# Tap sums on TensorE, filter copies shared with VectorE, sine tables between rows and Wo copies behind the x stores: a long convolution beside a recurrent attention

## The chip, the cores and the metric

The kernel runs on one core of a Trainium2 chip. The metric is device time in microseconds (us), the median of several executions; a profile of one execution gives its time by engine. Engines are TensorE (PE, with its weight loads as PEld), VectorE (DVE), ScalarE (ACT), GpSimd (POOL) and SyncE (SP). DMAs are issued from the queues of SP, ACT and POOL.

## The reference, cut to what matters

Two independent results lie side by side in the output: `A` in columns 0 to 1023, `B` in columns 1024 to 2047. Everything is bf16, with one batch and 2048 positions.

```python
# A: q, k, v [2048, 1024], shift_k [1024, 4], ssm_k [1024, 2048], ssm_D [1024]
k_pad   = pad(k, 3 zero rows in front)
k_shift = sum over t of k_pad[t:t+2048, :] * shift_k[:, 3-t]      # four taps of k
kv      = k_shift * v
y       = causal convolution over positions of kv with ssm_k (by FFT of length 4096)
A       = q * (y + kv * ssm_D)

# B: x [2048, 1024], mem0 [8, 1024], Wq, Wk, Wv [1024, 32 heads, 128], Wo [32, 128, 1024]
for s in range(64):                      # segments of 32 positions
    h = concat(mem, x[s])                # 8 + 32 rows
    q, k, v = h@Wq, h@Wk, h@Wv
    o = (masked softmax(q k^T / sqrt(128)) v) @ Wo
    mem, B[s] = o[:8], o[8:]             # the memory rows go on to the next segment
```

## The kernel before, in words

The program has two parts. `a_kernel` computes `A` in three stages and, while it does so, calls back into `b_kernel`, which prepares data for the 64 segments; then `b_kernel` runs the segments one after the other (from about 430 us to the end), streaming weights from a DRAM copy `WS`.

**Stage 1** (inside `with ExitStack() as c1`) runs 16 rows `t`. A row takes the 128 positions t, t+16, ... of all 1024 channels. In each row:

- eight TensorE transposes (L236) bring one slice of the filter `ssm_k` into PSUM (`k_tp`), and ScalarE copies it to SBUF as `kt` (L238). For row 0 VectorE adds `ssm_D` into it (L240);
- `stage1(kt, t, SK1)` multiplies it by two DFT matrices `F1h` (L220, four matmuls into two PSUM tiles `s_ps`, a pool of two), ScalarE copies each of the two results to SBUF (`s_sb`, L222, a pool of three), and SP stores them to DRAM (L223);
- `k` and `v` for two rows at a time are loaded in even rows (L244 on SP, L247 on POOL);
- VectorE forms the four taps of `k`: one product (L253), then three products (L256) each added to the sum `uacc` (L257), and multiplies the sum by `v` (L259) to `u`;
- `stage1(u, t, SU1)` does with `u` what was done with `kt`.

Before the rows come small tables, and among them four big sine tables that only stage 2 reads: `Mre` and `Mim` (L200 to L206), `Nre` and `Nim` (L207 to L213). VectorE forms the integer phases in a scratch tile `ints`, ScalarE applies Sin (in `act_sin`, L109), and POOL zeroes one stripe of each of `Mre` and `Mim` (L206).

`stage1_done` (L482) follows the rows: it transposes part of `x` into `XBT` (`make_xbt`; X loads held behind the stores of rows 3 to 6, its PSUM tiles from the pool `b_ps0`, tag `ps0`, two buffers) and runs `dense(0, 0)`, 16 times eight matmuls (L594) into `kb_ps`, which are also `ps0` tiles.

**Stage 2** has 17 sets of two units each; a unit gathers spectra of `u` and of the filter, multiplies them (DVE L327 to L330 and L334, POOL L333) and transforms back. **Stage 3** has 16 steps and writes `A`. After each of these 34 + 16 pieces `a_kernel` calls `fill()` (L629), which does one piece of `b_kernel`'s preparation: a store of finished projections, an x block (`x_block`, L565, with its store to `REC` on POOL at L575), one projection's matmuls, and, from piece `WO_COPY` = 27 on, one copy of a chunk of `Wo` to `WS`, from DRAM to DRAM, issued on POOL (L637). There are six such copies.

Outside the segments the order of the instructions on each engine is not that of the source: the framework sorts them by priority (order in the source) and readiness under its own model, hands out tile buffers as it goes, and fixes one order for each engine. `tc.issue_after(ins)` pins the instructions issued inside it behind `ins` in the order of the queue they share. The copies at L637 have nothing that they wait for, so they may be placed ahead of the piece that they were written in.

Of the kernel before, what the change touches and what calls it, by code (L numbers as in the profile page):

```python
# [9 lines left out]
BF = mybir.dt.bfloat16  # L10
F32 = mybir.dt.float32
I32 = mybir.dt.int32
ACT = mybir.ActivationFunctionType
ALU = mybir.AluOpType
# [16 lines left out]
PITCH = 2048  # L31


def a_kernel(ctx: ExitStack, tc, q, k, v, shift_k, ssm_k, ssm_D, outa, slot16, stage1_done, fill):
    nc = tc.nc
    S, D = 2048, 1024
    NP = 34
# [8 lines left out]
    ident = const.tile([128, 128], BF, name="a_ident")  # L46
    F1h = [const.tile([128, 128], BF, name=f"F1h{h}") for h in range(2)]
    G2h = [const.tile([128, 128], BF, name=f"G2h{h}") for h in range(2)]
    Mre = const.tile([128, NP, 64], BF, name="Mre")
    Mim = const.tile([128, NP, 64], BF, name="Mim")  # L50
    Nre = const.tile([128, NS, 128], BF, name="Nre")
    Nim = const.tile([128, NS, 128], BF, name="Nim")
# [4 lines left out]
    with ExitStack() as c1:  # L57
# [3 lines left out]
        wk = c1.enter_context(tc.tile_pool(name="a1_wk", bufs=3, side="right"))  # L61
# [46 lines left out]
        def act_sin(out_ap, a_int_ap, nbits, p0=0):  # L108
            nc.scalar.activation(out_ap, a_int_ap, ACT.Sin, bias=pi_col[p0:p0 + out_ap.shape[0], 0:1],  # L109
                                 scale=-2.0 * PI / (1 << nbits))  # L110
# [56 lines left out]
        SH = cw.tile([128, 4, 1024], BF, name="SH")  # L167
        for hf in range(4):
            pt = ps_big.tile([128, 1024], F32, tag="big", name="sh_ps")
            for e in range(2):  # L170
# [18 lines left out]
        nxr = cw.tile([128, 1], F32, name="nxr")  # L189
# [7 lines left out]
        nc.vector.tensor_scalar(out=w_f[:], in0=w_i[:], scalar1=kp[:, 0:1], scalar2=None, op0=ALU.add)  # L197
        nc.vector.tensor_tensor(out=aN0, in0=w_f[:].unsqueeze(2).to_broadcast([128, NS, 32]),
                                in1=kn2[:].unsqueeze(1).to_broadcast([128, NS, 32]), op=ALU.mult)
        for x, (M, n) in enumerate(((Mre, nxr), (Mim, nxi))):  # L200
            aM = phases(x).rearrange("p (a b) -> p a b", b=32)
            nc.vector.tensor_scalar(out=aM, in0=v_i, scalar1=p_n2[:, 0:1], scalar2=n[:, 0:1], op0=ALU.mult, op1=ALU.add)
            nc.vector.tensor_scalar(out=aM, in0=aM, scalar1=4095, scalar2=None, op0=ALU.bitwise_and)
            for (r0, c0) in [(0, 0), (64, 32)]:
                act_sin(M[r0:r0 + 64, :, c0:c0 + 32], aM[r0:r0 + 64], 12, r0)
            nc.gpsimd.memset(M[32:64, 0, :], 0.0)  # L206
        for y, (N, ph) in enumerate(((Nre, (1024, 0)), (Nim, (2048, 1024)))):  # L207
            aN = phases(y).rearrange("p (a b) -> p a b", b=64)
            for x in range(2):
                nc.vector.tensor_scalar(out=aN[:, :, 32 * x:32 * x + 32], in0=aN0, scalar1=ph[x], scalar2=None, op0=ALU.add)  # L210
            nc.vector.tensor_scalar(out=aN, in0=aN, scalar1=4095, scalar2=None, op0=ALU.bitwise_and)
            for (r0, c0) in [(0, 0), (32, 64), (64, 0), (96, 64)]:
                act_sin(N[r0:r0 + 32, :, c0:c0 + 64], aN[r0:r0 + 32], 12, r0)  # L213

        def stage1(u_tile, t, scratch):
            sb = wk.tile([128, 2, 1024], BF, tag="s1_sb", name="s1_sb")
            for h in range(2):
                pt = ps_big.tile([128, 1024], F32, tag="big", name="s1_ps")
                for hf in range(2):
                    nc.tensor.matmul(pt[:, hf * 512:(hf + 1) * 512], lhsT=F1h[h][:, :],  # L220
                                     rhs=u_tile[:, hf * 512:(hf + 1) * 512], start=True, stop=True)
                nc.scalar.copy(sb[:, h, :], pt[:])  # L222
            return nc.sync.dma_start(scratch.rearrange("m (r h) d -> r m h d", h=2)[t], sb[:])  # L223
# [8 lines left out]
        for t in range(16):  # L232
            pt = ps_t.tile([128, 1024], BF, tag="ktp", name="k_tp")
            for db in range(8):
                src = KS[:, db, :].rearrange("p (n r) -> p r n", r=16)[:, t, :]
                nc.tensor.transpose(pt[:, db * 128:(db + 1) * 128], src, ident[:])  # L236
            kt = wk.tile([128, 1024], BF, tag="kt", bufs=2, name="kt")
            nc.scalar.copy(kt[:], pt[:])  # L238
            if t == 0:
                nc.vector.tensor_tensor(out=kt[0:1, :], in0=kt[0:1, :], in1=Drow[0:1, :], op=ALU.add)  # L240
            stage1(kt, t, SK1)
            if t % 2 == 0:
                K0 = k0pool.tile([128, 2048], BF, tag="K0", name="K0")
                nc.sync.dma_start(K0[:], pair_rows(k, t))  # L244
                ktiles[t], ktiles[t + 1] = K0[:, 0:1024], K0[:, 1024:2048]
                Vp = io.tile([128, 2048], BF, tag="Vt", name="Vt")
                nc.gpsimd.dma_start(Vp[:], pair_rows(v, t))  # L247
            Vt = Vp[:, 1024 * (t % 2):1024 * (t % 2) + 1024]
            acc = wk.tile([128, 1024], BF, tag="uacc", bufs=2, name="uacc")
            for li, lag in enumerate((3, 2, 1, 0)):  # L250
                Kl = ktiles[t - lag]
                if li == 0:
                    nc.vector.tensor_tensor(out=acc[:], in0=Kl, in1=SH[:, lag, :], op=ALU.mult)  # L253
                else:
                    pr = wk.tile([128, 1024], BF, tag="prod", bufs=2, name="prod")
                    nc.vector.tensor_tensor(out=pr[:], in0=Kl, in1=SH[:, lag, :], op=ALU.mult)  # L256
                    nc.vector.tensor_tensor(out=acc[:], in0=acc[:], in1=pr[:], op=ALU.add)  # L257
            u = wk.tile([128, 1024], BF, tag="u", bufs=2, name="u")
            nc.vector.tensor_tensor(out=u[:], in0=acc[:], in1=Vt, op=ALU.mult)  # L259
            su_stores.append(stage1(u, t, SU1))  # L260

    stage1_done(su_stores)

# [126 lines left out]
def b_kernel(ctx: ExitStack, tc, x, mem0, Wq, Wk, Wv, Wo, outb, n_seg, run_a):  # L390
    nc = tc.nc
# [35 lines left out]
    def dram_chunk(ch):  # L427
        m, a, g = ch
        return Wo_v[a] if m == 3 else W_v[m][a, g]

    def dst_view(ap, ch):
        return ap.rearrange("p (hh d) -> p hh d", hh=2) if ch[0] == 3 else ap

    def stream_src(ch):
        return WS[ring_order.index(ch), :, 0:2048]
# [129 lines left out]
    def x_block(b):  # L565
        X_sb = loaded.pop(b)
        if b % 2 == 0:
            t = base.tile([128, 2048], BF, tag="wring3", name="xt")
            xts[b], xts[b + 1] = t[:, 0:1024], t[:, 1024:2048]
        tp = ps0.tile([128, 1024], BF, tag="ps0", name="xt_ps")  # L570
        for kc in range(8):
            nc.tensor.transpose(tp[:, kc * 128:(kc + 1) * 128], X_sb[:, kc * 128:(kc + 1) * 128], ident[:])
        xt = xts.pop(b).rearrange("p (s k t) -> p s k t", s=4, k=8)
        nc.vector.tensor_copy(xt, tp[:].rearrange("p (k j t) -> p j k t", k=8, j=4))
        nc.gpsimd.dma_start(REC[:, 4 * b:4 * b + 4, 0:256], xt.rearrange("p s k t -> p s (k t)"))  # L575

    xts = {}
    flip = [0]

    def evac(dst, src):  # L580
# [48 lines left out]
    def fill():  # L629
        store()  # L630
        n = units[0]
        units[0] += 1
        if n == 0:
            x_load(0)
        if n >= WO_COPY and wo_copies:
            ch = wo_copies.pop(0)
            nc.gpsimd.dma_start(dst_view(stream_src(ch), ch), dram_chunk(ch))  # L637
        if n % 3 == 2 and blocks:
            b = blocks.pop(0)
            x_block(b)  # L640
            if b % 2 and blocks:
                x_load(b + 1)
        if n >= 34 or n % 3 != 2:
            next(rest, None)

    run_a(slot16, stage1_done, fill)

    wres3 = ctx.enter_context(tc.tile_pool(name="b_wres", bufs=1, reuse_waits="tile"))
    for i, ch in enumerate(parts[1]):
# [413 lines left out]
@with_exitstack  # L1063
def kernel(
    ctx: ExitStack,
    tc: tile.TileContext,
    A_q: bass.AP,
    A_k: bass.AP,
    A_v: bass.AP,
    A_shift_k: bass.AP,  # L1070
    A_ssm_k: bass.AP,
    A_ssm_D: bass.AP,
    B_x: bass.AP,
    B_mem0: bass.AP,
    B_Wq: bass.AP,
    B_Wk: bass.AP,
    B_Wv: bass.AP,
    B_Wo: bass.AP,
    B_seg_len,
    out: bass.AP,  # L1080
):
    assert int(B_seg_len) == 32
    S = B_x.shape[1]
    n_seg = S // 32
    outa = out[0, :, 0:1024]
    outb = out[0, :, 1024:2048]
    def run_a(slot16, stage1_done, fill):
        with ExitStack() as ctx_a:
            a_kernel(ctx_a, tc, A_q[0], A_k[0], A_v[0], A_shift_k, A_ssm_k, A_ssm_D, outa, slot16, stage1_done, fill)

    with ExitStack() as ctx_b:
        b_kernel(ctx_b, tc, B_x[0], B_mem0[0],
                 B_Wq.rearrange("d h e -> d (h e)"), B_Wk.rearrange("d h e -> d (h e)"),
                 B_Wv.rearrange("d h e -> d (h e)"), B_Wo.rearrange("h e d -> (h e) d"),
                 outb, n_seg, run_a)
# [35 lines left out]
```

## Time and profile before

| what | value |
|---|---|
| median of 5 runs | 2161.12 us (2152.69 to 2165.71) |
| the profiled execution | 2165.19 us, its span 2163.4 us |
| busy in the span | PE 80%, PEld 43%, DVE 40%, ACT 30%, POOL 20% |
| DMA | 802.29 MB, mean 371 GB/s |
| stage 1: first ScalarE copy of a row's result to the last | 31.7 to 116.6 us |
| `dense(0, 0)` on TensorE | 120.3 to 152.1 us |
| stage 2's first set to its last store | 152 to 296 us |
| stage 3, then the remaining projections | 300 to 430 us |
| segments | 430 us to the end |

The busy shares are means over stages that differ: what the change touches lies in the first 300 us, so the windows of the profile there are what matters. In the lines of the profile an entry such as `L222 ACT CAST s_sb<-s_ps 128x1024 bf16<-128x1024 f32 x64` is a group: source line, engine, operation, written tile, read tile, shapes and count, then busy time and the mean time of one in ns. The duration of a VectorE or ScalarE instruction includes its way through the pipeline; back-to-back instructions start closer together than that, and sums are made with the distance between starts.

### The profile page before, as it was taken

The page shows a single profiled execution, that of the slowest core. Times are in us where ns is not written, and L with a number is a line of the kernel's source. Part 1 is how long each engine was busy: PE and PEld are TensorE (multiplying, and loading weights), DVE is VectorE, ACT ScalarE, POOL GpSimd, SP SyncE. Part 2 cuts the span into 40 slices and gives each one's busy share as a digit, 9 for nine tenths or more (in the row PEclk, how much of TensorE's full clock was granted, in tenths as well). Part 3 has the DMA queues.
Part 4 walks back from the last instruction along what each step waited for, and adds up shares of the span by engine and source line. Part 5 has one row for each costly group of instructions (what it writes and reads, how often), then busy time and mean ns, then how long its engine had stood idle before and what let it go on. Part 6 is the DMA issues. An engine that isn't in the chain of part 4 may idle for free. (4 is left out here: it accounts for less than half of the span.)

```text
span 2163.4 us, 81250 instructions
## 1 busy us (share of the span) xinstructions
PE 1721.3 (80%) x35605; PEld 928.6 (43%) x35636; DVE 873.1 (40%) x2691; ACT 648.3 (30%) x1139; POOL 424.7 (20%) x1100
## 2 busy tenths in 40 slices
PE   4587987977778878888788887888787888888886
PEld 2232333434444444444444444444444444444444
DVE  9826763133333333333333333333333333333332
ACT  7845531222222222222222222222222222222221
POOL 3013422311111111111112111111111111111111
PEclk9899999999999999999999999999999999999999
DMA  8999869999999999999999999999999999999997
GB/s 309 331 346 339 289 235 369 324 365 386 382 382 390 391 384 396 392 394 395 392 394 393 390 392 384 392 387 384 384 383 382 384 378 387 390 391 394 394 391 269
DMA packets 238311, 802.29 MB, mean 371 GB/s; under 512 B 34721, under 2 KB 34753, under 8 KB 237953
## 3 DMA queue, kind: packets, MB, share of 16 engines
q1 hardware_dynamic: 207186, 728.20, 87.9%
q0 software_dynamic: 25552, 58.39, 7.9%
q10 hardware_dynamic: 5216, 10.49, 1.3%
q8 instruction: 279, 4.57, 0.9%
q14 instruction: 78, 0.64, 0.1%
HBM read 737.56 MB, written 62.39 MB: 370 GB/s over the span
## 5 line engine op out<-in xcount | busy, mean ns | idle before, releaser
L907 PEld LDWEIGHTS <-rec 128*32 128x32 bf16 x12351 | 324.2, 95 | 468.7 <-issue 251.0
L907 PE MATMUL acc<-wring,rec 128*32 128x512 bf16 x3765 | 371.5, 383 | 138.0 <-DMA wring<-WS 121.5
L916 ACT CAST qkv_sb<-acc 128x512 bf16<-128x512 f32 x384 | 224.8, 585 | 654.3 <-PE acc L907 654.3
L993 PEld LDWEIGHTS <-OT 128*32 128x32 bf16 x8192 | 217.5, 97 | 177.7 <-issue 150.6
L993 PE MATMUL yacc<-wring,OT 128*32 128x256 bf16 x3072 | 154.2, 277 | 97.0 <-DMA wring<-WS 55.9
L907 PE MATMUL acc<-Wmid,rec 128*32 128x512 bf16 x3072 | 225.9, 383 | 0.0
L907 PE MATMUL acc<-Wres,rec 128*32 128x512 bf16 x2816 | 221.2, 380 | 0.0
L853 PEld LDWEIGHTS <-OTB 128*16 128x16 bf16 x4096 | 103.8, 89 | 104.5 <-issue 94.7
L979 ACT CAST OT<-OTp 128x512 bf16<-128x512 f32 x128 | 74.9, 585 | 245.1 <-PE OTp L971 245.0
L1009 DVE COPY KT<-tps 128x512 bf16<-128x512 bf16 x64 | 27.2, 425 | 295.3 <-PE tps L922 295.3
L980 DVE CAST OTB<-OTp 128x128 bf16<-128x128 f32 x128 | 37.3, 292 | 264.7 <-ACT OT L979 264.7
L808 POOL DMA_DIRECT2D rec<-REC x64 | 37.5, 586 | 522.1 <-issue 267.6
L755 DVE TENSOR_SCALAR wring<-OTp 128x384 int32<-128x384 int32 x126 | 112.3, 891 | 56.0 <-PE acc L907 49.8
L907 PE MATMUL acc<-pw,rec 128*32 128x512 bf16 x1544 | 131.2, 382 | 0.0
L883 POOL COPY KT<-rec 128x128 bf16<-128x128 bf16 x128 | 38.6, 302 | 419.7 <-PE SB L931 405.4
L937 DVE TENSOR_REDUCE mx<-SB 128x5 f32<-128x200 f32 x128 | 47.1, 368 | 180.5 <-PE SB L931 180.5
L868 POOL DMA_DIRECT2D out_dram<-YB x128 | 73.0, 577 | 237.4 <-DVE YB L866 217.2
L853 PE MATMUL SB<-wring,OTB 128*16 128x256 bf16 x1488 | 78.4, 274 | 39.4 <-DVE SB L832 32.4
L922 PE MATMUL tps<-ident,qkv_sb 128*128 128x128 bf16 x1024 | 101.2, 221 | 8.2 <-ACT qkv_sb L916 0.3
L922 PEld LDWEIGHTS <-qkv_sb 128*128 128x128 bf16 x1024 | 62.8, 97 | 104.7 <-ACT qkv_sb L916 64.6
L993 PE MATMUL yacc<-Wlate,OT 128*32 128x256 bf16 x2048 | 105.2, 275 | 1.8 <-issue 1.1
L1049 ACT CAST Y<-yacc 128x256 bf16<-128x256 f32 x64 | 23.8, 372 | 241.1 <-PE yacc L993 237.2
(231 smaller groups left out, 2654.2 us busy)
## 6 DMA issues: line engine op xcount, KB each, us to landing
wring<-WS SPq DMA_DIRECT2D x1215, 512.0 KB, 7.4
rec<-REC POOLq DMA_DIRECT2D x64, 192.0 KB, 6.0
SK<-s_sb SPq DMA_DIRECT2D x16, 512.0 KB, 4.2
SU<-s_sb SPq DMA_DIRECT2D x16, 512.0 KB, 5.3
Kg<-SK SPq DMA_DIRECT2D x32, 256.0 KB, 6.8
Ug<-SU SPq DMA_DIRECT2D x32, 256.0 KB, 6.9
REC<-stage POOLq DMA_DIRECT2D x16, 512.0 KB, 10.7
zt<-SZ SPq DMA_DIRECT2D x16, 512.0 KB, 7.6
```

Of the source, the lines that this page charges most:

```text
L755: nc.vector.tensor_scalar(out=dst, in0=src, scalar1=0, scalar2=None, op0=ALU.bitwise_or)
L808: nc.gpsimd.dma_start(rec[:], REC[:, s, :])
L853: nc.tensor.matmul(self.acc[32 * dq:32 * dq + W, x - o:y - o], lhsT=self.OTB[:, c, 4 * g + i, :], rhs=r, start=first and not self.seeded, ...
L868: nc.gpsimd.dma_start(bass.AP(outb.tensor, outb.offset + (SEG * NB * self.b + NX) * 2048 + 256 * dq, [[2048 * SEG, NB], [2048, 8], [1, 256 ...
L883: nc.gpsimd.tensor_copy(KT[:, :, :, 32:40], KBs[:, 128 * g:128 * g + 128].rearrange("p (c i t) -> p i c t", c=4, i=4))
L907: nc.tensor.matmul(self.acc[32 * c:32 * c + 32, x - 512 * c:y - 512 * c], lhsT=hT[:, kc, :], rhs=r, start=(kc == 0 and x == 512 * c), stop ...
L916: nc.scalar.copy(sb[:], self.acc[:])
L922: nc.tensor.transpose(tp[:, i * 128:(i + 1) * 128], sb[:, i * 128:(i + 1) * 128], ident[:])
L937: nc.vector.tensor_reduce(out=mx[:], in_=S, op=ALU.max, axis=AX.X)
L979: nc.scalar.copy(OT[:], o_view[:, :, :, 0:32])
L980: nc.vector.tensor_copy(OTB[:, :, 4 * g:4 * g + 4, 8 * j:8 * j + 8], o_view[:, :, :, 32:40])
L993: nc.tensor.matmul(yacc[32 * dq:32 * dq + 32, x - o:y - o], lhsT=OT[:, c, i, :], rhs=r, start=(h == 0 and x == o), stop=(h == 31), tile_po ...
```

## The change

It has four parts.

1. The four tap products are still formed on VectorE, now in halves of 512 channels, and are summed by TensorE: each product is multiplied by the identity matrix and accumulated in a PSUM tile `ks_ps`. VectorE then multiplies the sum in PSUM by `v`. The three additions to `uacc` per row are gone. The PSUM tiles come from `b_kernel`'s pool `b_ps0` (tag `ps0`, two buffers), which is handed over as `ps_sum`.
2. In odd rows the filter copy `kt` is made by VectorE instead of ScalarE.
3. The four sine tables become functions, called after rows 0, 1, 2 and 3.
4. Each Wo copy is issued behind the newest x block's store in POOL's queue.

```diff
+        def table_m(x, M, n):          # body as before, L201 to L206
...
+        def table_n(y, N, ph):         # body as before, L208 to L213
...
+        tables = [lambda: table_m(0, Mre, nxr), lambda: table_m(1, Mim, nxi),
+                  lambda: table_n(0, Nre, (1024, 0)), lambda: table_n(1, Nim, (2048, 1024))]
...
             kt = wk.tile([128, 1024], BF, tag="kt", bufs=2, name="kt")
-            nc.scalar.copy(kt[:], pt[:])
+            if t % 2:
+                nc.vector.tensor_copy(kt[:], pt[:])
+            else:
+                nc.scalar.copy(kt[:], pt[:])
...
-            acc = wk.tile([128, 1024], BF, tag="uacc", bufs=2, name="uacc")
-            for li, lag in enumerate((3, 2, 1, 0)):
-                Kl = ktiles[t - lag]
-                if li == 0:
-                    nc.vector.tensor_tensor(out=acc[:], in0=Kl, in1=SH[:, lag, :], op=ALU.mult)
-                else:
-                    pr = wk.tile([128, 1024], BF, tag="prod", bufs=2, name="prod")
-                    nc.vector.tensor_tensor(out=pr[:], in0=Kl, in1=SH[:, lag, :], op=ALU.mult)
-                    nc.vector.tensor_tensor(out=acc[:], in0=acc[:], in1=pr[:], op=ALU.add)
             u = wk.tile([128, 1024], BF, tag="u", bufs=2, name="u")
-            nc.vector.tensor_tensor(out=u[:], in0=acc[:], in1=Vt, op=ALU.mult)
+            sums = []
+            for hf in range(2):
+                cols = slice(512 * hf, 512 * hf + 512)
+                ps = ps_sum.tile([128, 512], F32, tag="ps0", name="ks_ps")
+                for li, lag in enumerate((3, 2, 1, 0)):
+                    pr = wk.tile([128, 512], BF, tag="prod", bufs=8, name="prod")
+                    nc.vector.tensor_tensor(out=pr[:], in0=ktiles[t - lag][:, cols], in1=SH[:, lag, cols], op=ALU.mult)
+                    nc.tensor.matmul(ps[:], lhsT=ident[:], rhs=pr[:], start=(li == 0), stop=(li == 3))
+                sums.append((cols, ps))
+            for cols, ps in sums:
+                nc.vector.tensor_tensor(out=u[:, cols], in0=ps[:], in1=Vt[:, cols], op=ALU.mult)
             su_stores.append(stage1(u, t, SU1))
+            if tables:
+                tables.pop(0)()
...
-        nc.gpsimd.dma_start(REC[:, 4 * b:4 * b + 4, 0:256], xt.rearrange("p s k t -> p s (k t)"))
+        rec_stores.append(nc.gpsimd.dma_start(REC[:, 4 * b:4 * b + 4, 0:256], xt.rearrange("p s k t -> p s (k t)")))
...
             ch = wo_copies.pop(0)
-            nc.gpsimd.dma_start(dst_view(stream_src(ch), ch), dram_chunk(ch))
+            with tc.issue_after(rec_stores[-1].ins):
+                nc.gpsimd.dma_start(dst_view(stream_src(ch), ch), dram_chunk(ch))
...
-    run_a(slot16, stage1_done, fill)
+    run_a(ps0, slot16, stage1_done, fill)
```

## The prediction

> **What bounds the kernel now.** I read the page first. Its chain of work that ended last lies in the segments and is made of DMA waits on `wring`; the change leaves the segments alone, so what it can give is an earlier start of them. I then asked for windows by stage over the first 430 us (columns: busy us of PE, PEld, DVE, ACT, POOL, then granted clock, DMA share, GB/s).
>
> ```profile
> span 2163.4 us, 81250 instructions
> ```
> ```profile
> 17.00:32.00 15.00, 2.36 (x9) 0.84 (x8) 14.38 (x24) 14.69 (x13) 6.80 (x12) 1.00 0.92 336
> 32.00:117.00 85.00, 51.69 (x231) 23.05 (x236) 70.84 (x129) 73.32 (x80) 5.11 (x11) 0.86 0.90 318
> 117.00:152.00 35.00, 31.88 (x142) 14.41 (x144) 3.46 (x5) 9.33 (x18) 0.56 (x1) 0.91 0.92 347
> ...
> 264.00:290.00 26.00, 24.42 (x117) 7.58 (x117) 21.91 (x39) 15.72 (x30) 13.93 (x14) 0.88 0.42 138
> ...
> 300.00:358.00 58.00, 40.76 (x175) 16.98 (x176) 23.02 (x23) 4.29 (x8) 13.82 (x17) 0.91 0.98 369
> ```
>
> The rows of stage 1 (32 to 117) hold three resources near full at once: ACT 86%, DVE 83%, DMA 90%. From 17 to 32 ACT and DVE are full, PE idle. After the rows PE is full (`dense`), late in stage 2 the DMA is 42% busy, in stage 3 it is the bound. To see which one ends stage 1, I read the timeline of ACT, then its groups over the first 130 us (idle time before each and its releasers behind the last bar), and the waits there.
>
> ```profile
> 17.10 2.42 ACT L109 ACTIVATE Mre<-ints,pi_col 64x1088 bf16<-64x1088 int32 x2 [0.67 <-DVE ints L203]
> 19.55 2.42 ACT L109 ACTIVATE Mim<-ints,pi_col 64x1088 bf16<-64x1088 int32 x2
> 22.00 4.83 ACT L109 ACTIVATE Nre<-ints,pi_col 32x1088 bf16<-32x1088 int32 x4
> 26.84 4.83 ACT L109 ACTIVATE Nim<-ints,pi_col 32x1088 bf16<-32x1088 int32 x4
> 31.70 1.93 ACT L222 CAST s_sb<-s_ps 128x1024 bf16<-128x1024 f32 x2
> ...
> 94.27 2.84 ACT L222 CAST s_sb<-s_ps 128x1024 bf16<-128x1024 f32 x3 [2.74 <-DMA SU<-s_sb]
> ```
> ```profile
> L222 ACT CAST s_sb<-s_ps 128x1024 bf16<-128x1024 f32 x64 | 61.1, 1039 | 11.7 <-DMA SU<-s_sb 5.7 <-PE s_ps L220 1.6 <-ACT kt L238 1.4
> L238 ACT COPY kt<-k_tp 128x1024 bf16<-128x1024 bf16 x16 | 16.1, 1051 | 2.4 <-PE k_tp L236 2.4
> ```
> ```profile
> PE s_ps L220 <- ACT s_sb L222: 22.2, 40, 3.1
> ```
>
> ACT cannot take a row's result before 31.7 because the sines stand first; its last row copy ends at 116.6. TensorE waited 40 times for ACT to empty an `s_ps` tile; VectorE's last `u` starts at 106.0, ten us before ACT ends. So ACT with its stores ends stage 1, VectorE close behind.
>
> **Part by part.** *Filter copies.* Copies of 1024 start 0.92 us apart on ACT (two in 1.93, one lasting 1.01). Eight leave it: 8 x 0.92 = 7.4 us, on the path. On VectorE a 128x1024 bf16 copy out of PSUM (`xt`, L574) starts 0.60 before the next: 4.8 us added there.
>
> *Sine tables.* Their 14.5 us stay on ACT; they move from ahead of the rows to among them, so row copies can begin at about 18 (TensorE's first `s_ps` matmuls are at 18.39) and the same work lies between. The sum doesn't change by the move alone: 80 copies x 0.92 + 14.5 = 88.1 us before, 80.7 after. ACT was idle 14.0 us between 14.5 and 116.6; at the same idle it ends at 14.5 + 80.7 + 14.0 = 109.2, **7.4 earlier**. There is no table reload to fear: the two ACT_TABLE_LOADs are at 2.62 and 7.05, and copies and sines alternate after them without another. The tables also issue POOL's two stripes (L206), for which POOL waited 5.05 and 1.74; behind them stood the first `v` loads at 20.9. Now these go first; later `v` loads queued behind a stripe have a row's time to spare.
>
> *Tap sums.* VectorE per row, before: eight passes of 1024, 0.602 apart = 4.82. After: eight products of 512 at 0.33 (distance after L334, same shape and types, with the engine's queue full) = 2.64, two products out of PSUM at 0.60 (L327 to L330) = 1.20, and 0.30 of filter copy: 4.14, so 16 x 0.68 = **10.9 us less**, from the engine that stands second.
>
> ```profile
> 277.13 0.69 DVE L328 TENSOR_TENSOR pb<-Uim_ps,Kim 128x512 bf16<-128x512 f32 x1
> 277.73 0.68 DVE L329 TENSOR_TENSOR pc<-Ure_ps,Kim 128x512 bf16<-128x512 f32 x1
> ```
>
> The Trainium skill, "VectorE: DVE Perf Modes" (the cycle table of its TRN2 errata section), gives 120 fixed cycles plus 512 for such a pass out of PSUM, an estimate of 0.66 us instead of the 0.60 read here; by it those 32 passes would cost 1.9 us more. The trace is taken.
>
> TensorE gets eight identity matmuls of 512 per row. At full clock such a matmul takes 0.21 (`s_ps` pairs last 0.59, a single one 0.38), four in a row from rest 1.86, that is 0.43 each.
>
> ```profile
> 46.47 1.86 PE L220 MATMUL s_ps<-kt,F1h 128*128 128x512 bf16 x4 [2.16 <-ACT kt L238]
> 87.91 0.59 PE L220 MATMUL s_ps<-u,F1h 128*128 128x512 bf16 x2 [0.32 <-ACT s_sb L222]
> ```
>
> A row then needs 16 x 0.21 + 8 transposes at 0.06 = 3.9 us warm, 7.7 cold, against 5.3 that a row takes now (84.9 us / 16). In the steady part (84 to 93 us) TensorE has about 0.33 free beside each of four copies and 0.25 at the filter copy: 1.6 us for 1.7 of tap sums. So I cost them at nothing, hidden beside ACT's copies; cold, the cover is gone and the row is 2.4 too long. The clock in the profile falls after idle gaps (0.74, 0.66 in the ten-us windows with waits of 2 us and more), and more work leaves fewer gaps. The Trainium skill, "TensorE: Matmul & The Clock Gate" (Part 1), has the gate release after about 3.4 us of steady work and halve the rate after an idle window; by it the early rows, still thin, run at half rate, against this change; by its halved rate all through, stage 1 would end at 18 + 16 x 7.7 = 141.
>
> Added wait: VectorE's pass out of PSUM waits for the last of four matmuls, and `u`, its `s_ps` matmuls and the next row's products queue behind it. Eight product buffers let the other half fill that gap. From the rows: nothing if filled, at most a matmul and two semaphore steps, some 0.7 x 16 = 11 us, if never. I take nothing, since VectorE has 1.2 us of each 5.3 us row spare.
>
> *Wo copies.* Now they run in the busy start:
>
> ```profile
> 22.52 0.69 POOL L637 DMA_DIRECT2D WS<-in_B_Wo_dram  x1
> ...
> 23.35 3.65 POOL L637 DMA_DIRECT2D WS<-in_B_Wo_dram  x5
> ```
>
> POOL's DMA queue (q0) takes 21.1% of the first 130 us for 18 transfers of 512 KB: 27.4 / 18 = 1.52 us each, 9.1 for six. DMA busy to 117 us is 15.5 + 13.8 + 76.5 = 105.8 (shares times windows); without them 96.7. At the same share, 0.904, that is done at 107: **10.0 earlier**. The copies go behind the stores of x blocks 8 and 9 (POOL at 264.6 and 270.9), into the 26 us with 15 us of idle DMA: nothing. If they slid on into stage 3, 9.1. On POOL six issues of 0.7 stand in front of `Yre` (L333), which idles 2 to 3 us before most of its passes: hidden, 4.3 if not.
>
> *The sum.* ACT says 7.4, DMA 10.0, VectorE more; ACT ends last but 6.1 of its idle is for stores, which the DMA's relief shortens. I take the middle, 8.7. `dense` (27 us of matmuls) and all behind it follow stage 1's end without slack of their own, so it reaches the segments whole: 2165.2 - 8.7 = 2156.5 for the profiled execution, which lay 4.1 above the median: **2152.4**.
>
> **The rivals.** *Full overlap* (0.15): tap sums keep the clock up and sines fill ACT's waits, until DMA is busy all the time: 96.7 + the first 2 = 98.7, 18 us earlier: 2143. For it: the idle gaps; against: three resources at 90% in the rows leave little buffer.
>
> *Swallowed* (0.29): the row is held by the stores. Three `s_sb` buffers, each held for two copies (1.84), an issue (0.32) and a landing (4.2 or 5.3), allow 6.9 x 2 / 3 = 4.6 us per row; if landings grow by 1.0 under the denser traffic, 5.3 as now, and the sines' time is won but partly lost again. Gain 0 to 6: 2155 to 2161. For it: `DMA SU<-s_sb` leads ACT's idle list.
>
> *Slower* (0.14): the PSUM pool. `ps0` also holds `make_xbt`'s blocks: the trace has the first two filled at 58.0 and 65.0 and emptied only from 116.4 on. If the sums' two buffers go to such a block, the rows stop until ACT gets round to emptying it. At a row each for four blocks, 4 x 5.3 = 21.2, less 8.7: 2173.6. It decides the sign from 2.2 us per block. Against: a starved ACT takes the block's copies (0.53 each) at once.
>
> That the sines don't move is possible too, as the order is worked out by readiness; the rest would still give most of the gain.
>
> **How the numbers follow.** Forecast 0.42, full overlap 0.15, swallowed 0.29, slower 0.14. About 0.3%, 6.5 us, is what a measurement of this kernel can tell from no change. Full overlap and nine tenths of the forecast case lie beyond it: 0.53; swallowed and the rest 0.33; slower 0.14. Half of the full overlap and half of the slower case stay outside the range: 2140 to 2167.
>
> **What would show it.** Right: the first `s_sb` copy near 18, sines between copies, the last row copy at 106 to 110, `s_ps` matmuls mostly at 0.21, no Wo copy before 260. Wrong: rows of 5.3 us or more with ACT waiting for `SU` stores or PE, `ks_ps` waiting on `XBT` copies, Wo copies in stage 3, or `dense` ending at 152 after an early stage 1.

## The result, and the profile after

| | median us | runs | lowest to highest |
|---|---|---|---|
| the kernel before, same chips | 2164.20 | 79 | 2151.89 to 2177.51 |
| the changed kernel | 2171.73 | 44 | 2163.40 to 2182.04 |

The ratio is 1.0035, with a 95% interval from 1.0026 to 1.0045: the change costs some 7.5 us where 8.7 were forecast as a gain. The profiled execution of the changed kernel took 2172.62 us.

Here are the windows of the changed kernel by stage, with the columns as before (busy us of PE, PEld, DVE, ACT, POOL, then granted clock, DMA share, GB/s).

```profile
span 2170.8 us, 81527 instructions
```
```profile
17.00:32.00 15.00, 11.52 (x50) 5.23 (x51) 12.95 (x32) 12.18 (x12) 1.90 (x6) 1.00 0.69 256
32.00:117.00 85.00, 66.77 (x338) 32.10 (x343) 61.31 (x148) 73.19 (x80) 3.90 (x8) 0.92 0.84 297
117.00:152.00 35.00, 31.33 (x124) 12.63 (x125) 4.88 (x18) 5.77 (x10) 1.18 (x4) 0.86 0.89 343
...
264.00:290.00 26.00, 24.93 (x131) 8.27 (x132) 21.93 (x40) 16.05 (x31) 18.02 (x20) 0.95 0.88 303
...
300.00:358.00 58.00, 40.97 (x182) 17.45 (x184) 22.86 (x23) 4.70 (x8) 13.86 (x17) 0.91 0.97 365
```

Every resource that the prediction counts was relieved as it said. VectorE's busy time from 17 to 117 falls from 85.22 to 74.26, DMA moves 256 and 297 GB/s where it moved 336 and 318, and TensorE works from the start. The Wo copies are in the window from 264 to 290, where the DMA share is now 0.88 instead of 0.42. POOL's timeline there:

```profile
265.48 0.78 POOL L585 DMA_DIRECT2D REC<-xt  x1
268.23 2.04 POOL L649 DMA_DIRECT2D WS<-in_B_Wo_dram  x3
...
282.46 1.34 POOL L649 DMA_DIRECT2D WS<-in_B_Wo_dram  x2
```

ScalarE's timeline (start, length) shows rows from 18 us on and the sines between them; the two group lines and the first wait below it are those shown of before (L222, L238 and L220 have become L226, L245 and L224), and the last line is VectorE's wait for the tap sums (total us, times, longest).

```profile
18.06 1.93 ACT L226 CAST s_sb<-s_ps 128x1024 bf16<-128x1024 f32 x2 [2.90 <-PE s_ps L224]
19.87 2.43 ACT L109 ACTIVATE Mre<-ints,pi_col 64x1088 bf16<-64x1088 int32 x2
...
47.17 4.84 ACT L109 ACTIVATE Nim<-ints,pi_col 32x1088 bf16<-32x1088 int32 x4
...
104.78 4.04 ACT L226 CAST s_sb<-s_ps 128x1024 bf16<-128x1024 f32 x4 [2.61 <-DMA SU<-s_sb]
...
111.27 1.96 ACT L226 CAST s_sb<-s_ps 128x1024 bf16<-128x1024 f32 x2
```
```profile
L226 ACT CAST s_sb<-s_ps 128x1024 bf16<-128x1024 f32 x64 | 60.7, 1034 | 16.0 <-DMA SU<-s_sb 6.9 <-PE s_ps L224 5.5 <-DMA SK<-s_sb 1.2
L245 ACT COPY kt<-k_tp 128x1024 bf16<-128x1024 bf16 x8 | 8.4, 1047 | 2.1 <-PE k_tp L240 2.0
```
```profile
PE s_ps L224 <- ACT s_sb L226: 9.6, 12, 2.2
...
DVE u L267 <- PE ks_ps L264: 6.1, 6, 1.8
```

The last row copy ends at 113.2, only 3.4 us earlier than the 116.6 of before. What follows is lost at once. This is `dense(0, 0)` on TensorE's timeline, first before, then after. The lines `Kre_ps` are stage 2's first set; one such matmul slips in early, and the start of the next, behind the long stretch, tells when `dense` is through.

```profile
120.26 4.26 PE L594 MATMUL kb_ps<-XBT,pw 128*128 128x512 bf16 x12 [0.67 <-ACT XBT L537]
125.19 0.61 PE L594 MATMUL kb_ps<-XBT,pw 128*128 128x512 bf16 x2 [0.67 <-DMA pw<-in_B_Wk_dram]
126.74 0.60 PE L594 MATMUL kb_ps<-XBT,pw 128*128 128x512 bf16 x2 [0.95 <-DMA pw<-in_B_Wk_dram]
127.42 0.38 PE L307 MATMUL Kre_ps<-Kg,Mre 128*64 128x512 bf16 x1
127.80 24.33 PE L594 MATMUL kb_ps<-XBT,pw 128*128 128x512 bf16 x109
152.06 0.40 PE L307 MATMUL Kre_ps<-Kg,Mre 128*64 128x512 bf16 x1
```
```profile
116.44 1.01 PE L605 MATMUL kb_ps<-XBT,pw 128*128 128x512 bf16 x2 [0.67 <-ACT XBT L547]
...
121.39 0.60 PE L605 MATMUL kb_ps<-XBT,pw 128*128 128x512 bf16 x2 [1.06 <-DMA pw<-in_B_Wk_dram]
122.91 0.93 PE L605 MATMUL kb_ps<-XBT,pw 128*128 128x512 bf16 x2 [0.92 <-DMA pw<-in_B_Wk_dram]
125.20 1.03 PE L605 MATMUL kb_ps<-XBT,pw 128*128 128x512 bf16 x2 [1.36 <-DMA pw<-in_B_Wk_dram]
...
126.74 25.89 PE L605 MATMUL kb_ps<-XBT,pw 128*128 128x512 bf16 x110
152.55 0.40 PE L317 MATMUL Kre_ps<-Kg,Mre 128*64 128x512 bf16 x1
```

`dense` starts 3.8 us earlier, then waits for its weights (`pw`) chunk by chunk until 126.7, runs its long stretch slower (110 matmuls in 25.89, against 109 in 24.33) and ends half a microsecond later than before. The weights come late because SP issues them late. SP's queue around the last stores of rows, before and then after:

```profile
110.22 0.42 SPq L551 DMA_DIRECT2D pw<-in_B_Wk_dram  x1
112.60 0.32 SPq L223 DMA_DIRECT2D SU<-s_sb  x1
114.44 0.32 SPq L223 DMA_DIRECT2D SK<-s_sb  x1
116.59 0.32 SPq L223 DMA_DIRECT2D SU<-s_sb  x1
116.96 1.72 SPq L551 DMA_DIRECT2D pw<-in_B_Wk_dram  x3
```
```profile
109.26 0.55 SPq L542 DMA_DIRECT2D pair<-in_B_x_dram  x1
110.94 0.33 SPq L227 DMA_DIRECT2D SK<-s_sb  x1
111.32 0.42 SPq L561 DMA_DIRECT2D pw<-in_B_Wk_dram  x1
113.26 0.32 SPq L227 DMA_DIRECT2D SU<-s_sb  x1
113.63 2.64 SPq L561 DMA_DIRECT2D pw<-in_B_Wk_dram  x4
```

Counting the `SU` stores ahead of each load in SP's timeline gives its place, which is fixed in the program. The eight loads stand behind rows 8, 10, 12, 13, 14, 16, 16, 16 before (rows counted from 1), and behind 9, 11, 12, 15, 16, 16, 16, 16 after; the X loads (`pair`) behind 4, 5, 8, 8 before and behind 4, 5, 14, 15 after. The pins at `K_LOAD` only say how early a load may be placed. X blocks 2 and 3 are held up by the tap sums: of the two kernels below that differ from these in part 1 alone, the one with sums has its X loads behind 4, 5, 13, 13, the one without behind 4, 5, 8, 8. That the shared PSUM tiles do it is likely, but wasn't tried by itself.

Up to the load of the first segment's record (398.66 us before, 398.44 after) the two executions are level, and their 7.4 us lie in the segments. `dense` and the segments both vary from execution to execution, so this pair can't place the loss.

### The profile page after: what moved, and what is told of

The parts are those of the page before. It is cut to its first block, busy times and chain, and to the rows that moved or that the text cites. A ratio compares the mean times of both kernels' runs of the same rounds, so it can differ in the third digit from the quotient of the medians.

```text
span 2170.8 us, 81527 instructions
## 1 busy us (share of the span) xinstructions
PE 1750.6 (81%) x35731; PEld 936.4 (43%) x35764; DVE 863.4 (40%) x2731; ACT 642.5 (30%) x1131; POOL 425.2 (20%) x1100
## 5 line engine op out<-in xcount | busy, mean ns | idle before, releaser
L919 PEld LDWEIGHTS <-rec 128*32 128x32 bf16 x12351 | 319.1, 96 | 471.0 <-issue 246.8
L919 PE MATMUL acc<-wring,rec 128*32 128x512 bf16 x3765 | 374.6, 385 | 136.6 <-DMA wring<-WS 118.4
L1005 PEld LDWEIGHTS <-OT 128*32 128x32 bf16 x8192 | 218.1, 97 | 180.1 <-issue 152.1
```

The source lines that it names most:

```text
L919: nc.tensor.matmul(self.acc[32 * c:32 * c + 32, x - 512 * c:y - 512 * c], lhsT=hT[:, kc, :], rhs=r, start=(kc == 0 and x == 512 * c), stop ...
L1005: nc.tensor.matmul(yacc[32 * dq:32 * dq + 32, x - o:y - o], lhsT=OT[:, c, i, :], rhs=r, start=(h == 0 and x == o), stop=(h == 31), tile_po ...
```

## The experiments

**First theory: the DRAM copy of the weights.** `WS`, which the segments stream, begins 16 MB higher in DRAM in the changed kernel, since another buffer is touched first. A tiny early transfer moves it down in the changed kernel, or up in the kernel before.

```diff
# after_ws_low: the changed kernel
+    nc.scalar.dma_start(WS[0, 0:1, 0:64], x[0:1, 0:64])
# before_ws_high: the kernel before
+    for scratch in (SK1, SU1):
+        nc.scalar.dma_start(scratch[0, 0:1, 0:64], k[0:1, 0:64])
```

> The changed kernel with one tiny DMA more at the start: 128 bytes are written to the first row of WS before anything else. The later copies overwrite them. Its effect is on placement: WS, which the segments stream from, lies at the DRAM offset that it has in the kernel before (0x14000) instead of 16 MiB higher (0x1014000). Theory A (placement): the seven us that the change lost lie in the segments and come from where WS lies; this kernel then takes as long as the kernel before or a little less, 2161 to 2166, ratio 0.998 to 1.001, and its segments last some 1731 us from the first queries to the end, not 1737. Theory B (something else in the change slows the segments, or its early part does): as the changed kernel, 2170 to 2173, ratio 1.003 to 1.004.

> The kernel before with two tiny DMAs more at the start (128 bytes each into the first rows of SK1 and SU1, overwritten later), which moves WS from DRAM offset 0x14000 to 0x1014000, where the changed kernel has it; nothing of the change itself is made. Theory A (placement): slower than the kernel before by the change's own loss, ratio 1.003 to 1.004, 2170 to 2173, all of it in the segments. Theory B: no difference, ratio 0.999 to 1.001.

Measured: 2170.77 us for the first, ratio 1.0035 [1.0015, 1.0056], the loss unchanged; 2167.72 for the second, 1.0016 [0.9995, 1.0037], which is no clear difference. The first shows that the loss is there without the high place of `WS`. The second decides nothing, since its interval holds both no change and the whole loss.

**Where the loss lies.** Both kernels with the segment loop cut to its first 4 of 64 turns; the other 60 segments are left out.

```diff
-        for s in range(n_seg):
+        for s in range(4):
```

> The kernel before with only the first 4 of the 64 segments run (the rest of B is left out); the preparation is whole. Its time is preparation plus 4 segments, about 545 us. It is to be set beside the same cut of the changed kernel. If the change's loss sits in the segments (theory A): the two cut kernels differ by under 2 us. If it sits in the preparation, and the one profile of each misleads (theory C): they differ by 6 to 8 us, the changed one longer. If stage 1's gain reaches the segments after all: the changed one is 3 to 9 us shorter.

> The changed kernel with only the first 4 of the 64 segments run. Theory A (loss in the segments): within 2 us of the cut kernel before. Theory C (loss in the preparation): 6 to 8 us longer. Swallowed gain: row copies end near 113 instead of 117, and projections of stage 1's end still finish near 152.

Measured: 552.90 (549.05 to 553.42) and 562.68 (559.49 to 566.30), 9.8 us apart: a loss of at least the full kernel's size lies ahead of the fifth segment. From here on cuts are compared with cuts. They ran on several chips, on which the uncut kernel before had medians of 2163.4 to 2164.7.

**The held Wo copies.** The changed kernel without the pin on them.

```diff
-            with tc.issue_after(rec_stores[-1].ins):
-                nc.gpsimd.dma_start(dst_view(stream_src(ch), ch), dram_chunk(ch))
+            nc.gpsimd.dma_start(dst_view(stream_src(ch), ch), dram_chunk(ch))
```

> The changed kernel without its fourth part: the Wo copies aren't pinned and run in stage 1 again. If the hold is free as forecast and frees stage 1's DMA, this is 0 to 9 us slower than the changed kernel, 2172 to 2181. If the copies' new place late in stage 2 is what cost the time, it is 3 to 8 us faster, 2164 to 2169. If neither matters because the segments set the difference, 2170 to 2173.

Measured: 2170.10, ratio 1.0026 [1.0009, 1.0044] to before. To the changed kernel's 2171.73 that is no clear difference: the hold is worth nothing that can be measured, in either direction.

**The tap sums and the place of the loads.** Two cuts undo or do part 1 alone, and two move the loads alone.

```diff
# after_pw_early_s4: the changed kernel
-X_LOAD, K_LOAD = 3, 7
+X_LOAD, K_LOAD = 3, 2
# before_pw_late_s4: the kernel before
-            with tc.issue_after(su[K_LOAD + kc].ins):
+            with tc.issue_after(su[(8, 10, 11, 14, 15, 15, 15, 15)[kc]].ins):
# after_no_tap_s4: the changed kernel, the products and adds of before in place of ks_ps
# before_tap_s4: the kernel before, with the ks_ps products and matmuls
```

> The changed kernel with the tap sums undone (products and adds on VectorE again), everything else of the change kept, cut to the first 4 of 64 segments; to be read beside the cuts of before (552.90 us) and of the changed kernel (562.68 us). Without the sums no X block is held back and fewer weight loads are left behind the last row. Theory (late weight loads in front of the first dense pass): about 550, dense ends near 146 us; the half copies on VectorE alone take ScalarE's 7 us off the rows or are swallowed (548 to 553). Rival (the other parts cost the time): 558 or more, dense still ending near 155.

> The kernel before with the tap sums alone, cut to the first 4 of 64 segments. The sums hold the X blocks back to after row 13, but only two weight loads of the first dense pass come after the last rows, as before. Theory (the weight loads' place is the cost): 552 to 555, close to the cut of before. Rival (the sums themselves slow the rows, through VectorE waiting on TensorE or the other way round): 558 to 562, with the last row copy over 118 us.

> The changed kernel with the weight loads of the dense stage tied to rows from the second on rather than from the seventh (one constant, 7 to 2), cut to the first 4 of 64 segments: the loads then stand behind rows 3, 4, 5, 10, 11, 13, 16 and 16. Theory (late weight loads): back by 4 to 6 us, 556 to 559, and the first dense pass of K waits for no more than one load. Rival (rows and sums): 562 as the uncut constant gives, since the loads only take their queue's time elsewhere.

> The kernel before, its weight loads of the dense stage tied to later rows (they stand behind rows 10, 11, 12, 15 and four behind row 16, much as in the changed kernel), cut to the first 4 of 64 segments, nothing else changed. Theory (late weight loads): 557 to 560, 4 to 7 us over the cut of before, with the first dense pass waiting on three or four loads. Rival (rows and sums): 553, as before.

Measured, with the places and times read from one profiled execution each (the column `dense` ends is the first `Kre_ps` behind the long stretch):

| cut | `pw` loads behind rows | last row copy starts | first `kb_ps` | `dense` ends | median us |
|---|---|---|---|---|---|
| before_s4 | 8, 10, 12, 13, 14, 16, 16, 16 | 111.1 | 115.9 | 147.7 | 552.90 |
| after_s4 | 9, 11, 12, 15, 16, 16, 16, 16 | 116.3 | 120.6 | 158.0 | 562.68 |
| after_no_tap_s4 | 9, 10, 11, 12, 13, 13, 15, 16 | 117.2 | 91.7 | 152.9 | 553.20 |
| before_tap_s4 | 8, 9, 10, 12, 12, 14, 16, 16 | 114.2 | 118.4 | 148.8 | 553.54 |
| after_pw_early_s4 | 3, 4, 5, 10, 11, 13, 16, 16 | 111.6 | 116.8 | 147.5 | 549.47 |
| before_pw_late_s4 | 10, 11, 12, 15, 16, 16, 16, 16 | 116.8 | 121.5 | 158.4 | 560.26 |

The tap sums alone cost nothing (553.54 against 552.90), and taking them out of the changed kernel brings it back to before (553.20). Neither the sums alone nor the other parts alone put four loads behind the last row; only the whole change does. What costs the time is that place: with all of the change kept and one constant altered, the cut is 13.2 us faster, over twice the 4 to 6 expected, and the kernel before with its loads placed late is 7.4 us slower, with the same waits. TensorE's timeline of before_pw_late_s4, then of after_pw_early_s4:

```profile
121.47 4.25 PE L594 MATMUL kb_ps<-XBT,pw 128*128 128x512 bf16 x10 [0.67 <-ACT XBT L537]
127.61 0.60 PE L594 MATMUL kb_ps<-XBT,pw 128*128 128x512 bf16 x2 [1.90 <-DMA pw<-in_B_Wk_dram]
129.22 1.03 PE L594 MATMUL kb_ps<-XBT,pw 128*128 128x512 bf16 x2 [1.00 <-DMA pw<-in_B_Wk_dram]
131.15 1.03 PE L594 MATMUL kb_ps<-XBT,pw 128*128 128x512 bf16 x2 [0.90 <-DMA pw<-in_B_Wk_dram]
...
158.41 0.40 PE L307 MATMUL Kre_ps<-Kg,Mre 128*64 128x512 bf16 x1
```
```profile
117.61 5.12 PE L605 MATMUL kb_ps<-XBT,pw 128*128 128x512 bf16 x14 [0.22 <-issue]
...
123.19 24.33 PE L605 MATMUL kb_ps<-XBT,pw 128*128 128x512 bf16 x110
147.45 0.40 PE L317 MATMUL Kre_ps<-Kg,Mre 128*64 128x512 bf16 x1
```

The waits on `pw` are gone, the long stretch takes 24.33 again, and `dense` is through 10.5 us before that of after_s4. after_no_tap_s4 was expected to end `dense` near 146 and ended it at 152.9. In its order of instructions `dense` starts among the rows, at 91.7, and TensorE waits there for `pw` four times (1.3, 4.2, 2.8 and 2.9 us), with the last rows' `s_ps` matmuls behind these waits in its timeline.

**The same at full length.** The early constant in both kernels, and the changed kernel with every weight load ahead of the store of row 14 (`X_LOAD, K_LOAD = 2, 0`).

> The changed kernel at full length with the weight loads of the first dense pass tied to rows from the second on (7 to 2). Theory (the loss is the late weight loads): the cut of it stood 13.2 us below the cut of the changed kernel and 3.4 below the cut of before, so 2171 - 13 = 2158 to 2161, 3 to 6 below before. Rival (something behind the fourth segment takes part of it back): 2164 or more.

> The kernel before at full length with the same constant (7 to 2), which in its program puts the loads behind rows 3, 6, 11, 12, 13, 14, 16, 16 and X blocks 2 and 3 behind rows 6 and 10. Theory: before had only a small wait on these loads (1.3 us in the cut), so 2162 to 2165, within 2 us of before; the changed kernel with the constant is then faster than this one by 3 to 5, which is what the change is worth when the loads are out of its way. Rival (early loads are worth the same to both, the change itself gives nothing): 2159 to 2161.

> The changed kernel at full length with the weight loads tied to rows from the first on and the X loads to rows from the third (constants 3, 7 to 2, 0): all eight weight loads then stand ahead of the store of row 14. Theory: no load is left behind the rows, so the first dense pass starts on the last X block and waits for none: 2156 to 2160. Rival (more transfers among the first rows hold the row stores up and push the rows out by what the loads gave): 2161 to 2166.

Measured: 2166.61, ratio 0.9998 [0.9974, 1.0021]; 2163.70, 0.9995 [0.9975, 1.0016]; 2162.44, 0.9985 [0.9962, 1.0007]. The changed kernel with early loads stands level with the kernel before, and its interval lies below that of the changed kernel (1.0026 to 1.0045): the loss is undone. The gain of 3.4 that its cut shows, and the 2158 to 2161 expected from it, doesn't stand out at full length.

The full-length profiles agree with the cuts when all are taken together. Three have the late places of the changed kernel (after, after_ws_low, after_no_hold): `dense` ends at 152.6, 154.9 and 157.0, and the first record is loaded at 398.4, 401.0 and 404.3. Two have the places of before (before, before_ws_high): 152.1 and 149.7, and 398.7 and 393.1. With early weight loads (after_pw_early, before_pw_early, after_pw_first) `dense` ends at 150.0, 149.0 and 148.0, and the first record is loaded at 397.9, 396.9 and 390.4.

**Did the rows get shorter at all?** Three cuts: the constant in the kernel before, all weight loads early, and four buffers for the row result in place of three.

```diff
# after_early_s1x4_s4: the changed kernel with K_LOAD = 2
-        k0pool = c1.enter_context(tc.tile_pool(name="a1_k0", bufs=4, side="right"))
+        k0pool = c1.enter_context(tc.tile_pool(name="a1_k0", bufs=3, side="right"))
-            sb = wk.tile([128, 2, 1024], BF, tag="s1_sb", name="s1_sb")
+            sb = wk.tile([128, 2, 1024], BF, tag="s1_sb", bufs=4, name="s1_sb")
```

> The kernel before with the weight loads tied to rows from the second on, cut to the first 4 of 64 segments; beside the cut of the changed kernel with the same constant (549.47 us) it says what the change itself is worth when its loads do not stand in its way. Theory (the rows did get shorter by a few us, and late loads hid it): 551 to 554, so the change is worth 2 to 4. Rival (the rows did not get shorter at all, the constant alone gave the gain): 548 to 550.

> The changed kernel with the weight loads tied to rows from the first on and the X loads to rows from the third (no load left behind the rows), cut to the first 4 of 64 segments. Theory (loads behind the rows are the only thing between the last row and the first dense pass): 546 to 549. Rival (loads among the first rows slow them by as much): 550 to 553.

> The changed kernel with the early weight loads (7 to 2) and four buffers for the row result instead of three (paid for by three K buffers instead of four), cut to the first 4 of 64 segments; its loads stand behind rows 3, 4, 6, 10, 12, 13, 16, 16. If the row stores with three buffers are what keeps the rows at 5.3 us each (ScalarE waits for an SK or SU store about ten times, some 15 us in all): 543 to 546 against 549.47, with the last row copy ending near 106. If the rows are held by TensorE's order or by VectorE, or the time of the stores only moves: 549 to 551.

Measured: 550.82 (549.42 to 552.27), 551.81 (546.10 to 554.05) and 548.40 (544.51 to 550.24). With the same early constant in both (the places still differ), the change is worth 550.82 - 549.47 = 1.3 us, and the runs of the two overlap. after_pw_first_s4 waits for no weight at all:

```profile
116.62 1.04 PE L545 MATMUL xbt_ps<-ident,pair 128*128 128x128 bf16 x8 [3.28 <-DMA pair<-in_B_x_dram]
118.33 29.98 PE L605 MATMUL kb_ps<-XBT,pw 128*128 128x512 bf16 x125 [0.67 <-ACT XBT L547]
```

but in its profile the rows end later (last row copy at 113.2), and its median lies no lower than that of after_pw_early_s4. So each theory of that run holds in half: no wait for weights was left, and the time didn't fall. What TensorE waits for ahead of `dense` is now the last X block (`pair`, 3.28 us). The fourth buffer took ScalarE's waits for stores away and shortened nothing; the last row copy starts at 112.9. There was little to take: these waits come to 3.3 us in the view of after_pw_early_s4, not the 15 that the expectation names. ScalarE's waits from 18 to 113 us (total us, times, longest), first of after_pw_early_s4, then of after_early_s1x4_s4:

```profile
ACT s_sb L226 <- PE s_ps L224: 7.6, 7, 2.3
...
ACT s_sb L226 <- DMA SK<-s_sb: 2.0, 1, 2.0
...
ACT s_sb L226 <- DMA SU<-s_sb: 1.3, 2, 0.9
```
```profile
ACT s_sb L226 <- PE s_ps L224: 12.0, 11, 2.7
```

What ScalarE no longer waits for stores it waits for TensorE. Last, the tap sums taken out of that version again, with `X_LOAD` raised from 3 to 8 (weight loads behind rows 3, 4, 5, 8, 12, 13, 14, 15), as a cut and at full length, and that version itself at full length.

> As the cut of the changed kernel with early loads and four result buffers (548.40 us, rows end near 113), but the tap products added on VectorE again; loads behind rows 3, 4, 5, 8, 12, 13, 14, 15 and X loads behind rows 10, 11, 12 and after; first 4 of 64 segments. That kernel's ScalarE waited 12 us for s_ps and 0 for stores. If the sums on TensorE are what ScalarE then waits for (64 more pairs of matmuls among the s_ps): rows end near 107 and the cut takes 542 to 545. If VectorE's adds or the order of one row's steps hold the rows as well: 548 to 552, rows ending at 112 or later.

> The changed kernel at full length with early weight loads (7 to 2), four result buffers and three K buffers; the best cut so far (548.40, 4.5 under the cut of before). If the preparation's gain arrives whole: 2158 to 2161, against 2164 before and 2171.7 for the changed kernel. If later stages take it back: 2163 to 2167.

> The same without the tap sums, at full length. If the sums on TensorE held the rows: 2153 to 2156. If VectorE's adds or the order hold them as well: 2161 to 2166.

Measured: the cut 550.95 (544.75 to 553.50), its last row copy at 113.7. The rows didn't get shorter, but that doesn't clear the sums: with the additions back VectorE is busy 87.2 of the 95 us from 18 to 113, where it was 74.8 with the sums. At full length that version takes 2162.01 with the sums, ratio 0.9989 [0.9963, 1.0014], and 2162.16 without them, 0.9985 [0.9964, 1.0006]. None of the versions tried is measurably faster than the kernel before.

## Why the prediction was wrong

**The step that failed first** is in the sum: "`dense` (27 us of matmuls) and all behind it follow stage 1's end without slack of their own". `dense` follows two things, the last X block and its own weight loads. In the kernel before it already waited for the second (0.67 and 0.95 us at 125.19 and 126.74, on lines that the prediction didn't read), with three loads issued behind the last row's store. The change gave SP's order another shape, four loads behind the last row and one just ahead of it. The last wait for a load ends at 125.2, 12 us after the last row copy, where it was 126.7 and 10 us. So `dense` is through at 152.6 after a stage 1 that ended 3.4 us earlier, which the prediction itself names as a sign of being wrong. In the cuts the 10.3 us between the ends of `dense` (147.7 and 158.0) are 4.6 of later start, 4.0 more from the first `kb_ps` to the long stretch (7.5 before: 115.94 to 123.45; 11.5 after: 120.55 to 132.02), and 1.7 of a slower long stretch. With early loads the changed kernel's cut has none of the three (116.8, 6.4 us, 24.33), with late ones the kernel before has them all. That the place of the loads decides the loss is shown, by the medians in both directions. How much of it runs through the rows is not: in these four profiles late loads go with rows that end some 5 us later, no wait shows why, and at full length the last row copy ends anywhere from 110 to 117, in the changed kernel's own profile (113.2) ahead of the kernel before (116.6).

**The second step that failed** is the 8.7 itself. Its terms arrived: ScalarE's groups lost 77.2 - 69.1 = 8.1 us of busy time (7.4 by starts), VectorE 10.96 (10.9 said), DMA its six copies. But "at the same idle it ends at 109.2" didn't hold. From 14.15 to 113.2 ScalarE is idle 17.8 us by starts where it was 14.0, so half of the relief turned to waiting in this profile; in the medians with the early constant in both kernels 1.3 us are left of it. Waits for stores of `SU`, which "the DMA's relief shortens", went from 5.7 to 6.9, and waits for `s_ps` from 1.6 to 5.5. The wait for the tap sums, which the prediction took as nothing, cost VectorE 6.1 us; whether that held ScalarE is not shown. DMA's 10.0 was worth nothing that can be measured: after_no_hold puts the copies back into the rows and takes 2170.10. A resource at 90% isn't a bound by that alone. Here four engines pass a row round in an order fixed for each, and where a fourth buffer took the waits for stores away, waits for TensorE stood in their place. What holds the rows at their length stays open.

**The rivals.** *Slower* named the pool `ps0`, shared with `make_xbt`, but not what came of it: the sums don't wait for X blocks, the X loads stand behind rows 14 and 15. These places cost nothing by themselves, since after_pw_early_s4 keeps them and takes 549.47. That its time of 2173.6 came near is luck: the price is paid through late weights and not through stopped rows. *Swallowed* was right that the rows would hardly shorten, but its cause isn't borne out: with a fourth buffer ScalarE waits for no store, and the rows are no shorter. *Full overlap* didn't occur.

**What was right.** The first row copy at 18.06, sines between copies, Wo copies in the idle window at no cost, and the price of the tap sums on TensorE: most pairs of `ks_ps` last 0.59 us, and the cut with the sums alone is level with before. The early rows ran cold, as the rule weighed there would have them, only in part. The first four `s_ps` matmuls, at 17.01, take 1.87 us as they do in the kernel before (1.86), although the clock of that window reads 1.00; from 26.1 on pairs last 0.59. Between 40 and 50, behind a wait of 2.41 us, the clock is 0.66 and three `ks_ps` take 1.49. The rule shows at the start of `dense` too. The windows from 112 to 126 us, of the cut of before and then of the cut of the changed kernel:

```profile
112.00:126.00 14.00, 10.41 (x45) 4.80 (x45) 0.61 (x1) 5.33 (x11) 0.56 (x1) 0.76 1.01 371
```
```profile
112.00:126.00 14.00, 10.39 (x34) 3.85 (x33) 1.41 (x13) 8.63 (x13) 0.80 (x3) 0.53 0.95 303
```

The granted clock reads 0.76 and 0.53, but the second window holds the end of the rows up to 120.5. From the first `kb_ps` to the long stretch alone (115.94 to 123.45 and 120.55 to 132.02) it is 0.76 and 0.65. In after_s4 the first eight `kb_ps`, ahead of any wait for weights, take 3.57 us (0.45 each). Amid the waits, from 126 to 132, the clock is 0.72, and the long stretch starts slow: its first 30 matmuls take 8.34 us (0.28 each), all 112 26.04 us where before_s4 takes 24.35 (0.217 each). The Trainium skill, "TensorE: Matmul & The Clock Gate" (Part 1), gives 426.7 ns from start to start cold and 215.7 warm for such a matmul; the 0.217 of these rows agrees with the second, and the 0.45, which includes the end of the last of eight, with the first.

## What to carry to other kernels

Before you carry an earlier end of one stage on to the next, list everything that the first instruction of the next stage needs, with the queue that issues it and its place in that queue; a load that stands behind the last store of the stage can turn the gain into a wait. A change in one engine's work can reorder prefetches on a queue that the diff never mentions, so the order of issue is worth comparing whenever an order is worked out by readiness. And a loss of this kind costs one constant to test: move the loads and measure again.

## What the runs showed that was not expected

- Where four loads of 512 KB are issued in one go, loads land later: the median from issue to landing of the eight `pw` loads is 8.4 us in after_s4 against 6.4 in before_s4 and 6.2 in after_pw_early_s4, at a DMA share of 0.95 to 1.01 about the end of the rows.
- One profile says little about the total here. In after_early_s1x4 `dense` ends at 143.0, nine us ahead of the kernel before, and yet that execution took 2166.59. From the load of segment 1's record to that of the last one, ten full-length profiles range from 1711.3 to 1728.9 us, more than everything this change moves, at a DMA share of 1.00 in most of it. The kernels with tap sums have 1717.8 to 1724.6 and one 1728.5, those without 1711.3 to 1717.1 and one 1728.9. Whether that is more than chance, and so where the cuts' last 3 us stay at full length, is open.
